# An attention-and-MLP kernel in which TensorE waits on its own products' counts instead of on a nop of another engine

## The chip, the cores and the metric

One core of a Trainium2 chip. Its engines are TensorE (PE in the profile, with weight loads as PEld), VectorE (DVE), ScalarE (ACT), GpSimd (POOL) and SyncE (SP), which issues nearly all DMA transfers here. Each engine works through a queue of its own in order; engines wait for one another through semaphores, which an instruction counts up when it completes. The metric is the time of one execution on the device in microseconds (us), the median of several runs. Engine names with a q, such as ACTq or PEldq, are the engine's queue: instructions that only wait, count or issue.

## What is computed

A transformer layer in which attention and MLP stand side by side, for 2048 tokens of width 512, 32 heads of width 16 and an MLP of width 1792, with fp32 input and output. Cut to what matters:

```
xn = layernorm(x)                                   # x: 1 x 2048 x 512
q, k, v = split_heads(xn @ wqkv)                    # 32 heads of 16
p = softmax(q @ k^T * 16 ** -0.5)                   # 2048 x 2048 for each head
attn = merge_heads(p @ v) @ wo
mlp = gelu_tanh(xn @ w1 + b1) @ w2 + b2             # 512 -> 1792 -> 512
out = x + attn + mlp
```

## The kernel before

**Number formats.** Operands of most products are split into a high and a low half-precision part; a dense product over one piece of its inner dimension is then three products (`PAIRS`, L155): high by high, high by low, low by high. Scores have the parts stacked in the inner dimension. Probabilities and V are fp32, and a product of those goes through the array in two passes.

**Stages.** A head of some 137 us prepares inputs and the first projections. Then one loop of units runs until close to the end. A unit has the attention work of one group of four heads, one block of 512 queries and one tile of 128 keys, and takes its dense work from a generator: first the other projections of q, k and v, then the MLP (for each of four blocks of 512 tokens: the first layer in 14 groups, then the second layer in four), and last the output projection, each as *groups* that fill one accumulator bank. Scores run 20 units (`LEAD`) ahead of the exponentials and P·V, because every row's maximum must be known before its exponentials: `s_half` (L214) makes scores with queries on partitions and VectorE takes their maximum (L226); `e_half` (L262) makes the same scores transposed, the maxima being in the operand as extra rows, and ScalarE takes the exponential from the bank (L273); `v_half` (L276) multiplies it with V.

**One block.** A unit has two half units, here *blocks*. The order is written by hand (a manual schedule: each engine's instructions stand in the order of the program). In a block TensorE gets

1. score products S, transposed scores T, S, T (one head each, in alternation on array rows 0 to 63 and 64 to 127);
2. four P·V products of an earlier unit's exponentials, on one row side `r`: each covers 64 keys and has 32 output columns of its own;
3. dense products on the other row side, `1 - r`, by `dense` (L532): three or four calls of `tiled` (L171) by the group's pace, each of four products with 32 columns of their own, so 12 or 16. `SLOW` is three calls in each block, `MEAN` three and four by turns, `FAST` four. The MLP's first layer alternates `SLOW` and `FAST` groups, its second layer has `SLOW` for the first two token blocks and `MEAN` for the last two; projections and output projection are `FAST`. A group ends after 6 blocks (`FAST`) or 8 (`SLOW`) in the first layer, after 28 (`SLOW`) or 24 (`MEAN`) in the second. In the block in which a new accumulation of P·V begins, dense products come first.

Both accumulators, one bank for P·V and one for the dense group, are fed from one row side in one block and from the other side in the next. Products on different row sides run at the same time on the array, so a block's P·V and dense products must not start before the last ones of the block before have finished: the order of instructions on TensorE alone does not give that.

**How that is kept.** All products go through `product` (L165), which keeps the newest one in `newest`. At the end of a block `unit` (L551) issues a nop (L579) on ScalarE or VectorE, whichever has the smaller backlog by the planner's account, and makes it depend on `newest` (L580). In the next block the first P·V or dense product (`fence[0]`, set at L566, used at L167) is made to wait for the nop. Whether a product counts for other readers (the reduction, the exponential, a buffer's next writer) is settled by the framework, which gives each instruction with a dependant on another engine its count.

**Buffers and loads the change touches.** `pe` (L271), the exponentials, has ten buffers; one is free once the P·V products that read it are done. `wc` (three buffers, weights of the first layer), `xb` (one buffer, a block of tokens) and `oc` (output projection) are read by dense products and loaded by SP. `stg` (L464) stages projections before they go to memory, `wo_l` (L95, loaded at L875) has a piece of the output weights for the tail.

Of the kernel before, what the change touches and what calls it, by code (L numbers as in the profile page):

```python
# [8 lines left out]
F32 = mybir.dt.float32  # L9
F16 = mybir.dt.float16  # L10
# [7 lines left out]
P = 128  # L18
S = 2048
D = 512  # L20
# [4 lines left out]
NC = D // P  # L25
NF = F // P
QB = 512
# [20 lines left out]
def layer_kernel(ctx: ExitStack, tc: tile.TileContext, x, wqkv, wo, w1, b1, w2, b2, out):  # L48
    nc = tc.nc
# [3 lines left out]
    def pool(stack, name, bufs=1, space=None):  # L53
        kw = {} if space is None else {"space": space}
        return stack.enter_context(tc.tile_pool(name=name, bufs=bufs, **kw))

    const = pool(ctx, "const")
# [34 lines left out]
    nc.gpsimd.memset(vv[:, :, 0:H * VW].rearrange("p t (h e) -> p t h e", e=VW)[:, :, :, DH], 1.0)  # L92
    nc.gpsimd.memset(vv[:, :, H * VW:], 0.0)
    wo_s = const.tile([P, 2, NC, D], F16, name="wo_s")
    wo_l = const.tile([64, 2, D], F16, name="wo_l")  # L95
    sexp = const.tile([P, 4], F32, name="sexp")

    mnegs = [const.tile([P, 32], F32, name=f"mneg{i}") for i in range(2)]
# [55 lines left out]

    PAIRS = ((0, 0), (0, 1), (1, 0))  # L155

    AFTER = mybir.DependencyInfo(mybir.DependencyClass.Sync, mybir.DependencyReason.DATA)
    fence, newest = [None], [None]

    backlog = {"act": 0, "dve": 0}  # L160

    def given(engine, ns):
        backlog[engine] += ns

    def product(*args, **kw):  # L165
        newest[0] = nc.tensor.matmul(*args, **kw)  # L166
        if fence[0] is not None:  # L167
            tc.add_manual_dep(newest[0].ins, fence[0].ins.name, AFTER, reason="other rows")
            fence[0] = None

    def tiled(dst, lhs, rhs, start, stop):  # L171

        for j in range(0, P, 32):
            product(dst[j:j + 32], lhs[:, j:j + 32], rhs, start=start, stop=stop)


    mt_of, ptiles, pv_of = {}, {}, {}
# [36 lines left out]
    def s_half(u, n):  # L214

        t, i = divmod(u, 16)
        g, qb = divmod(t, NQB)
        qt, kb = divmod(i, 4) if t else (i % 4, i // 4)
        if t not in mt_of:
            mt_of[t] = work.tile([P, 4, 4, 4], F32, name="mt", bufs=2)  # L220
        ks, qs = kst[g % 2], qst[g % 2]
        p, a = divmod(n, 2)
        r = slice(64 * a, 64 * a + 62)
        s = banks("S")
        tiled(s, qs[p][qb][r, qt * P:(qt + 1) * P], ks[p][kb][r, :], True, True)
        nc.vector.reduce_max(mt_of[t][:, n, qt, kb:kb + 1], s, axis=AX.X)  # L226
        given("dve", 600)

# [33 lines left out]
    def e_half(u, n):  # L262

        p, a = divmod(n, 2)
        t, kt = divmod(u, 16)
        g, qb = divmod(t, NQB)
        st = banks("T")
        r = slice(64 * a, 64 * a + 64)
        k0 = (kt % 4) * P
        tiled(st, kst[g % 2][p][kt // 4][r, k0:k0 + P], qst[g % 2][p][qb][r, :], True, True)  # L270
        pe = work.tile([P, QB], F32, name="pe", bufs=10)  # L271
        ptiles[u, n] = pe
        nc.scalar.activation(pe, st, AF.Exp, scale=sexp[:, g // 2:g // 2 + 1])  # L273
        given("act", 580)

    def v_half(u, a):  # L276

        t, kt = divmod(u, 16)
        g, qb = divmod(t, NQB)
        if kt == 0 and a == 0:  # L280
            pv_of[t] = hold("V", "S")
        pv = pv_of[t][0]
        r = slice(64 * a, 64 * a + 64)
        for h in (2, 3, 0, 1):
            c = (4 * g + h) * VW
            product(pv[32 * h:32 * h + 32, :], vv[r, kt, c:c + 32], ptiles[u, h][r],
                    start=(kt == 0 and a == 0), stop=(kt == 15 and a == 1))

    def v_end(u):
# [90 lines left out]
    class Group:  # L380
# [15 lines left out]
        def product(self, side):  # L396

            if self.bank is None:
                self.bank, self.key = self.alloc()
            lhs, rhs = self.prods[side % 2][self.at[side % 2]]()  # L400
            start = self.first and self.at == [0, 0]
            if side == 2:
                self.at = [min(self.at[0] + 1, n) for n in self.n]
                nc.tensor.matmul(self.bank, lhs, rhs, start=start, stop=self.last and self.over())  # L404
                return
            r = slice(64 * side, 64 * side + 64)
            self.at[side] += 1
            tiled(self.bank, lhs[r], rhs[r], start, self.last and self.over())

        def over(self):  # L410
            return self.at == self.n
# [40 lines left out]
    def project(m, w, sb, wh, bank, early=False):  # L452

        prods = [lambda c=c, i=i, j=j: (wh[:, w, i, c, :], xt[:, j, c, sb * QB:(sb + 1) * QB])
                 for c in range(NC) for i, j in PAIRS]

        dst = qk_d[w, m * P:(m + 1) * P, :, sb * QB:(sb + 1) * QB]

        def finish(pj):
            def put():  # L460
                nc.sync.dma_start(dst[:, w:w + 2, :], stg)
                nc.sync.dma_start(dst[:, 2 - 2 * w, :], stg[:, 0])

            stg = work.tile([P, 2, QB], F16, name="stg", bufs=2)  # L464
            given("act", 600)
            if early or (w == 1 and not m):
                nc.scalar.activation(stg[:, 0], pj, AF.Copy)
                nc.vector.tensor_tensor(stg[:, 1], pj, stg[:, 0], op=ALU.subtract)
            else:
                pf = ph.tile([P, QB], F32, name="pf", bufs=2)  # L470
                nc.scalar.activation(pf, pj, AF.Copy)
                if not m:
                    nc.scalar.activation(stg[:, 0], pj, AF.Copy)
                    nc.gpsimd.tensor_tensor(stg[:, 1], pf, stg[:, 0], op=ALU.subtract)
                else:
                    hi = lambda: nc.gpsimd.tensor_scalar(stg[:, 0], pf, 1.0, 0.0, op0=ALU.mult, op1=ALU.add)
                    lo = lambda: nc.gpsimd.tensor_tensor(stg[:, 1], pf, stg[:, 0], op=ALU.subtract)
                    later(1, lambda: pooled((620, hi), (1160, lo), (0, lambda: later(1, put, True))), True)
                    return

            put()

        return Group(prods, bank, finish)
# [62 lines left out]
                    cur[0].product(side)  # L546
        ended()

    passed_by = [None]

    def unit(gen):  # L551


        u = pos[0]
        e = u - LEAD
        if u == LEAD and cur[0] is not None:
            burst(gen, cur[0].left())
        pos[0] += 1
        for a in range(2):
            for b in range(2 * a, 2 * a + 2):  # L560
                if u < NU:
                    s_half(u, b)
                if 0 <= e < NU:
                    e_half(e, b ^ 1)
            if e >= 0:
                fence[0] = passed_by[0]  # L566

                w, r = (e - 2, 1) if a == 0 else (e - 1, 0)
                live = 0 <= w < NU
                new = r == 0 and w % 16 == 0  # L570
                if live and not new:
                    v_half(w, r)
                dense(gen, 1 - r)
                if live and new:
                    v_half(w, r)

                for k in backlog:
                    backlog[k] = max(0, backlog[k] - HALF)
                passed_by[0] = (nc.vector if backlog["dve"] < backlog["act"] else nc.scalar).nop()  # L579
                tc.add_manual_dep(passed_by[0].ins, newest[0].ins.name, AFTER, reason="block")  # L580
                if live and r == 1:
                    v_end(w)
                ended()
        if u < NU:
            s_end(u)
        if u < LEAD:
            burst(gen, LFILL[u - 16])
        tick()
# [9 lines left out]
    with ExitStack() as st1:  # L598
# [240 lines left out]
        def prepare():  # L839
# [20 lines left out]
            for n in range(16):  # L860
                v = fetch(16 + n)
                while not ended[0]:
                    yield
                ended[0] = False

                def then(wh=None, n=n):
                    ended[0] = True
                    if n < 7:
                        for a in range(2):
                            for l in range(2):  # L870
                                nc.sync.dma_start(w1_d[2 * n + a][:, l], wh[:, l, :, a * P:(a + 1) * P])
                    elif n < 14:
                        nc.sync.dma_start(w2_d[:, :, 2 * n - 14:2 * n - 12, :], wh)
                    elif n == 15:
                        nc.sync.dma_start(wo_l, wo_s[64:128, :, NC - 1, :])  # L875

                if n >= 14:
                    i = 2 * (n - 14)
                    split_steps(wo_s[:, 0, i:i + 2, :], wo_s[:, 1, i:i + 2, :], v, inv[:, 9:10], then)
                    continue  # L880
                wh = ph.tile([P, 2, 4, W] if n < 7 else [P, 2, 2, D], F16, name="wsp", bufs=2)
                k = n if n < 7 else 8
                split_steps(wh[:, 0], wh[:, 1], v, inv[:, k:k + 1], lambda wh=wh, then=then: then(wh))
# [150 lines left out]
        flush()  # L1034
    with ExitStack() as st3:
        p3 = pool(st3, "ph3")

        blocks = {}

# [64 lines left out]
```

## Time and profile before

| | |
|---|---|
| median of 3 runs | 1587.66 us (1586.63 to 1590.76) |
| the profiled execution | 1592.59 us |
| its span in the trace | 1590.8 us |
| granted TensorE clock, mean | 0.992 |
| blocks that end with a nop | 1027, from 137.3 to 1568.0 us |

The page of the profile begins with each engine's busy time, then shows the chain of work that ended last. Busy time is an average: matmul records overlap, since products on different pieces of the array run side by side, and an engine that is busy 97% of the span can still wait for something in every block. Rows of the timeline have start and length in us, then engine, line, operation, tiles (out<-in), partitions and elements, and the count of instructions gathered in the row; in brackets stands the engine's idle time before and what ended it. In views of waits the numbers are the total us, the times and the longest.

### The profile page before, as it was taken

The page shows a single profiled execution, that of the slowest core. Times are in us where ns is not written, and L with a number is a line of the kernel's source. Part 1 is how long each engine was busy: PE and PEld are TensorE (multiplying, and loading weights), DVE is VectorE, ACT ScalarE, POOL GpSimd, SP SyncE. Part 2 cuts the span into 40 slices and gives each one's busy share as a digit, 9 for nine tenths or more (in the row PEclk, how much of TensorE's full clock was granted, in tenths as well). Part 3 has the DMA queues.
Part 4 walks back from the last instruction along what each step waited for, and adds up shares of the span by engine and source line. Part 5 has one row for each costly group of instructions (what it writes and reads, how often), then busy time and mean ns, then how long its engine had stood idle before and what let it go on. Part 6 is the DMA issues. An engine that isn't in the chain of part 4 may idle for free.

```text
span 1590.8 us, 86996 instructions
## 1 busy us (share of the span) xinstructions
PE 1535.3 (97%) x38915; PEld 807.7 (51%) x38915; DVE 1424.0 (90%) x2388; ACT 1378.9 (87%) x2254; POOL 668.7 (42%) x742
## 2 busy tenths in 40 slices
PE   8997998999999999999999999999999999999998
PEld 4433554545555555555455555555555555554443
DVE  7896987989999999999899999999999999999901
ACT  4315997989999999999899999999999999999893
POOL 3113586727773111677411157681116775211000
PEclk9999999999999999999999999999999999999999
DMA  6466375361112111121111111221112110103222
GB/s 204 136 210 210 108 190 184 124 197 53 44 54 64 35 34 31 55 60 46 46 38 48 33 53 41 61 67 33 33 46 59 41 34 15 39 23 97 91 95 82
DMA packets 120256, 123.78 MB, mean 78 GB/s; under 512 B 38988, under 2 KB 90572, under 8 KB 119880
## 3 DMA queue, kind: packets, MB, share of 16 engines
q1 hardware_dynamic: 119880, 118.21, 24.6%
q8 instruction: 304, 4.98, 1.3%
q14 instruction: 72, 0.59, 0.1%
HBM read 80.61 MB, written 37.34 MB: 74 GB/s over the span
## 4 chain that ended last, share of the span: by engine, by line
PE 80%; DVE 10%; DMA 4%; POOL 2%; issue 2%; SPq 1%; ACT 1%; DVEq 0%; ACTq 0%; POOLq 0%
PE pV L166 25%; PE pD L166 18%; PE pT L166 17%; PE pS L166 16%; DVE mt L226 6%; DVE hh L955 2%; PE pD L404 1%; DMA wch<-in_B_w_dram 1%; PE pT L404 1%; DVE amx L614 1%; DMA dn<-den_d 1%; PE pT L497 1%; ACT pe L273 0%; DMA m_d<-mhl 0%; DMA xb<-xn_d 0%
## 5 line engine op out<-in xcount | busy, mean ns | idle before, releaser
L226 DVE TENSOR_REDUCE mt<-pS 128x1 f32<-128x512 f32 x2048 | 1293.2, 683 | 59.4 <-PE pS L166 34.3
L273 ACT ACTIVATE pe<-pT,sexp 128x512 f32<-128x512 f32 x2048 | 1270.1, 686 | 77.5 <-PE pT L166 27.9
L166 PE MATMUL pV<-pe,vv 64*32 64x512 f32 x8192 | 1083.3, 599 | 1.9 <-ACTq L579 0.8
L166 PE MATMUL pT<-qst,kst 64*32 64x512 f16 x8192 | 708.1, 379 | 11.3 <-DMA qst<-m_d 8.2
L166 PE MATMUL pS<-kst,qst 62*32 62x512 f16 x8192 | 640.9, 379 | 28.0 <-DVE mt L226 24.1
L166 PEld LDWEIGHTS <-qst 62*32 62x32 f16 x8192 | 271.5, 92 | 253.2 <-issue 123.0
L166 PEld LDWEIGHTS <-kst 64*32 64x32 f16 x8192 | 290.9, 91 | 209.4 <-issue 80.2
L166 PE MATMUL pD<-w_s,g 64*32 64x512 f16 x5376 | 365.4, 379 | 0.0
L166 PE MATMUL pD<-xb,wc 64*32 64x512 f16 x5376 | 360.9, 378 | 0.2 <-issue 0.2
L166 PEld LDWEIGHTS pV<-pe,vv 64*32 64x32 f32 x8192 | 177.0, 105 | 122.4 <-ACTq L579 25.4
L166 PEld LDWEIGHTS <-wc 64*32 64x32 f16 x5376 | 117.4, 92 | 46.0 <-issue 2.3
L166 PEld LDWEIGHTS <-g 64*32 64x32 f16 x5376 | 106.9, 92 | 44.2 <-issue 0.7
L166 PE MATMUL pD<-xt,wqk_h 64*32 64x512 f16 x1920 | 127.4, 381 | 0.7 <-issue 0.7
L973 POOL TENSOR_TENSOR xa<-xa,yt 128x512 f32<-128x512 f32 x16 | 20.4, 1276 | 242.9 <-ACT yt L971 242.9
L935 POOL TENSOR_TENSOR t<-hh 128x512 f32<-128x512 f32 x56 | 58.2, 1039 | 119.3 <-DVE hh L955 117.8
L324 POOL TENSOR_TENSOR osb<-osb,rb 128x512 f32<-128x512 f32 x31 | 39.8, 1284 | 157.0 <-DMA rb<-den_d 115.1
L250 POOL TENSOR_SCALAR mhl<-msb 64x64 f16<-64x64 f32 x32 | 7.6, 236 | 178.4 <-DVE msb L247 178.4
L937 POOL TENSOR_TENSOR t<-t,hh 128x512 f32<-128x512 f32 x56 | 71.7, 1280 | 4.7
L930 POOL TENSOR_TENSOR t<-t,hh 128x512 f32<-128x512 f32 x56 | 71.5, 1277 | 4.7
L932 POOL TENSOR_TENSOR g<-t,g 128x512 f16<-128x512 f32 x56 | 65.1, 1163 | 4.4
L166 PE MATMUL pD<-wo_s,oc 64*32 64x512 f16 x768 | 50.8, 378 | 0.8 <-issue 0.8
L166 PEld LDWEIGHTS <-wqk_h 64*32 64x32 f16 x1920 | 43.0, 92 | 16.7 <-issue 1.9
(138 smaller groups left out, 868.0 us busy)
## 6 DMA issues: line engine op xcount, KB each, us to landing
wch<-in_B_w_dram SPq DMA_DIRECT2D x28, 512.0 KB
wc<-w_d SPq DMA_DIRECT2D x56, 256.0 KB
qk_d<-stg SPq DMA_DIRECT2D x32, 256.0 KB
rb<-den_d SPq DMA_DIRECT2D x124, 64.0 KB
kst<-qk_d SPq DMA_DIRECT2D x128, 48.0 KB
qst<-qk_d SPq DMA_DIRECT2D x128, 48.0 KB
xs<-in_A_x_dram SPq DMA_DIRECT2D x16, 256.0 KB
qk_d<-stg SPq DMA_DIRECT2D x32, 128.0 KB
```

The lines of the kernel that those rows point to most:

```text
L166: newest[0] = nc.tensor.matmul(*args, **kw)
L226: nc.vector.reduce_max(mt_of[t][:, n, qt, kb:kb + 1], s, axis=AX.X)
L273: nc.scalar.activation(pe, st, AF.Exp, scale=sexp[:, g // 2:g // 2 + 1])
L324: pooled((1280, lambda: nc.gpsimd.tensor_tensor(osb, osb, rb, op=ALU.mult)), (620, lambda: nc.gpsimd.tensor_scalar(ot[:, 0], osb, 1.0, 0.0 ...
L404: nc.tensor.matmul(self.bank, lhs, rhs, start=start, stop=self.last and self.over())
L497: nc.tensor.matmul(pj, xt[:, i, c, t * P:(t + 1) * P], wh[j][:, c, :], start=(n == 0), stop=(n == 11))
L930: (1280, lambda: nc.gpsimd.tensor_tensor(t1, t1, hh, op=ALU.mult)),
L932: (1160, lambda: nc.gpsimd.tensor_tensor(g[:, 1, f, :], t1, g[:, 0, f, :], op=ALU.subtract)),
L935: pooled((1040, lambda: nc.gpsimd.tensor_tensor(t1, hh, hh, op=ALU.mult)), (620, lambda: nc.gpsimd.tensor_scalar(t1, t1, 1.0, 1.0 / GELU_A ...
L937: (1280, lambda: nc.gpsimd.tensor_tensor(t1, t1, hh, op=ALU.mult)),
L955: nc.vector.tensor_scalar(hh, hp, scale, bias, op0=ALU.mult, op1=ALU.add)
L973: add = lambda: nc.gpsimd.tensor_tensor(xa, xa, yt, op=ALU.add)
```

## The change

The nop of the other engine goes. Each P·V product carries a key of its kind and head, each dense product one of its kind and column piece, score products none. At the end of a block `leave` takes the newest product of each key, so the four last P·V and the four last dense products, and makes each count a semaphore `turns` up by one when it completes; it does so only where the accumulation goes on in the next block. In the next block `enter` puts one instruction on TensorE's queue that waits until `turns` has reached the number counted so far. It is also declared to the framework as the point after which those products are done; who reuses their operands' buffers waits for that point. The exponentials get twelve buffers instead of ten. `stg` moves to the pool of the first stage, and `wo_l` with its load to the last stage.

```diff
-    wo_l = const.tile([64, 2, D], F16, name="wo_l")
...
-    AFTER = mybir.DependencyInfo(mybir.DependencyClass.Sync, mybir.DependencyReason.DATA)
-    fence, newest = [None], [None]
...
-    def product(*args, **kw):
-        newest[0] = nc.tensor.matmul(*args, **kw)
-        if fence[0] is not None:
-            tc.add_manual_dep(newest[0].ins, fence[0].ins.name, AFTER, reason="other rows")
-            fence[0] = None
-
-    def tiled(dst, lhs, rhs, start, stop):
+    turns = tc.alloc_semaphore("turns")
+    counted, waits, newest = [0], [[]], {}
+
+    def product(key, *args, **kw):
+
+        p = nc.tensor.matmul(*args, **kw)
+        if key[0] is not None:
+            newest[key] = p
+
+    def leave(user, goes_on):
+
+        for key in [k for k in newest if k[0] == user]:
+            p = newest.pop(key)
+            if goes_on:
+                p.then_inc(turns, 1)
+                tc.no_tile_sem_insts.add(p.ins.name)
+                counted[0] += 1
+                waits[0].append(p)
+
+    def enter():
+
+        if waits[0]:
+            group = f"turn{counted[0]}"
+            for p in waits[0]:
+                tc.add_to_no_dep_group(group, p.ins)
+            w = nc.tensor.wait_ge(turns, counted[0])
+            tc.declare_fence(w.ins, group=group)
+            waits[0] = []
+
+    def tiled(user, dst, lhs, rhs, start, stop):
 
         for j in range(0, P, 32):
-            product(dst[j:j + 32], lhs[:, j:j + 32], rhs, start=start, stop=stop)
+            product((user, j), dst[j:j + 32], lhs[:, j:j + 32], rhs, start=start, stop=stop)
...
-        pe = work.tile([P, QB], F32, name="pe", bufs=10)
+        pe = work.tile([P, QB], F32, name="pe", bufs=12)
...
-            product(pv[32 * h:32 * h + 32, :], vv[r, kt, c:c + 32], ptiles[u, h][r],
+            product(("V", h), pv[32 * h:32 * h + 32, :], vv[r, kt, c:c + 32], ptiles[u, h][r],
...
-            stg = work.tile([P, 2, QB], F16, name="stg", bufs=2)
+            stg = ph.tile([P, 2, QB], F16, name="stg", bufs=2)
...
-                fence[0] = passed_by[0]
+                enter()
...
+                for user, goes_on in (("V", live and not (r == 1 and w % 16 == 15)),
+                                      ("D", cur[0] is not None and not cur[0].over())):
+                    leave(user, goes_on)
                 for k in backlog:
                     backlog[k] = max(0, backlog[k] - HALF)
-                passed_by[0] = (nc.vector if backlog["dve"] < backlog["act"] else nc.scalar).nop()
-                tc.add_manual_dep(passed_by[0].ins, newest[0].ins.name, AFTER, reason="block")
...
-                    elif n == 15:
-                        nc.sync.dma_start(wo_l, wo_s[64:128, :, NC - 1, :])
...
         p3 = pool(st3, "ph3")
+        wo_l = p3.tile([64, 2, D], F16, name="wo_l")
+        nc.sync.dma_start(wo_l, wo_s[64:128, :, NC - 1, :])
```

More of the change, by code (lines that the diff above doesn't have):

```diff
@@ L224, in s_half @@
         s = banks("S")
-        tiled(s, qs[p][qb][r, qt * P:(qt + 1) * P], ks[p][kb][r, :], True, True)
+        tiled(None, s, qs[p][qb][r, qt * P:(qt + 1) * P], ks[p][kb][r, :], True, True)
         nc.vector.reduce_max(mt_of[t][:, n, qt, kb:kb + 1], s, axis=AX.X)
@@ L269, in e_half @@
         k0 = (kt % 4) * P
-        tiled(st, kst[g % 2][p][kt // 4][r, k0:k0 + P], qst[g % 2][p][qb][r, :], True, True)
-        pe = work.tile([P, QB], F32, name="pe", bufs=10)
+        tiled(None, st, kst[g % 2][p][kt // 4][r, k0:k0 + P], qst[g % 2][p][qb][r, :], True, True)
+        pe = work.tile([P, QB], F32, name="pe", bufs=12)
         ptiles[u, n] = pe
@@ L407, in product @@
             self.at[side] += 1
-            tiled(self.bank, lhs[r], rhs[r], start, self.last and self.over())
+            tiled("D", self.bank, lhs[r], rhs[r], start, self.last and self.over())
         def over(self):
@@ L547, in land @@
         ended()
-    passed_by = [None]
     def unit(gen):
```

## The prediction

> **What bounds the kernel now.** The page's busy shares and its chain of waits came first.
>
> ```profile
> span 1590.8 us, 86996 instructions
> PE 1535.3 (97%) x38915; PEld 807.7 (51%) x38915; DVE 1424.0 (90%) x2388; ACT 1378.9 (87%) x2254; POOL 668.7 (42%) x742
> PE 80%; DVE 10%; DMA 4%; POOL 2%; issue 2%; SPq 1%; ACT 1%; DVEq 0%; ACTq 0%; POOLq 0%
> PE pV L166 25%; PE pD L166 18%; PE pT L166 17%; PE pS L166 16%; DVE mt L226 6%; DVE hh L955 2%; PE pD L404 1%; DMA wch<-in_B_w_dram 1%; PE pT L404 1%; DVE amx L614 1%; DMA dn<-den_d 1%; PE pT L497 1%; ACT pe L273 0%; DMA m_d<-mhl 0%; DMA xb<-xn_d 0%
> ```
>
> The products of L166 carry 76% of the chain. But four of them run side by side on pieces of the array, so 97% busy does not say that the array is full. What matters is the period of a block (half a unit), so I then counted exponentials (two to a block) by stage.
>
> ```profile
> 160.00:317.20 157.20, 129.78 (x211) 0.98 0.51 152
> 333.10:472.20 139.10, 120.17 (x195) 1.00 0.26 77
> 473.50:621.90 148.40, 138.62 (x223) 1.00 0.15 43
> 622.90:759.70 136.80, 120.39 (x195) 1.00 0.19 52
> 760.50:914.60 154.10, 138.37 (x223) 0.98 0.14 42
> 915.70:1053.30 137.60, 120.55 (x195) 1.00 0.18 52
> 1054.10:1182.30 128.20, 118.83 (x191) 1.00 0.14 42
> 1183.30:1319.00 135.70, 120.44 (x195) 1.00 0.16 45
> 1319.80:1448.10 128.30, 118.87 (x191) 1.00 0.09 24
> 1448.80:1463.10 14.30, 13.71 (x25) 1.00 0.30 91
> 1465.60:1501.10 35.50, 30.15 (x49) 1.00 0.41 132
> 1513.50:1563.90 50.40, 47.51 (x77) 1.00 0.26 84
> ```
>
> The columns are the stretch, its length, ScalarE's busy time and count at the exponential L273, the granted clock, DMA share and rate. The first stretch is the projections. The four with x195 are the MLP's first layer (549.2 us, 390 blocks, 1.41 us each). The two with x223 are its second layer at the slow pace (302.5 us, 223 blocks, 1.36), the two with x191 the same at the mean pace (256.5 us, 191 blocks, 1.34). The last three are attention and output projection.
>
> What holds a block at these periods is seen in the timeline, rows being start, length, engine and operation: a block with twelve dense products, one with sixteen, and two with none.
>
> ```profile
> 563.65 0.63 PE L166 MATMUL pV<-pe,vv 64*32 64x512 f32 x4
> 563.68 0.61 PE L166 MATMUL pD<-w_s,g 64*32 64x512 f16 x8
> ...
> 564.10 0.61 PE L166 MATMUL pV<-pe,vv 64*32 64x512 f32 x4
> 564.12 0.39 PE L166 MATMUL pD<-w_s,g 64*32 64x512 f16 x4
> ...
> 564.94 0.63 PE L166 MATMUL pV<-pe,vv 64*32 64x512 f32 x4
> ```
>
> ```profile
> 1546.92 0.64 PE L166 MATMUL pV<-pe,vv 64*32 64x512 f32 x4
> ...
> 1546.95 0.61 PE L166 MATMUL pS<-wo_s,oc 64*32 64x512 f16 x8
> ...
> 1548.25 0.63 PE L166 MATMUL pV<-pe,vv 64*32 64x512 f32 x4
> ```
>
> ```profile
> 1460.27 3.07 DVE L226 TENSOR_REDUCE mt<-pS 128x1 f32<-128x512 f32 x5
> ...
> 1460.72 0.63 PE L166 MATMUL pV<-pe,vv 64*32 64x512 f32 x4
> ...
> 1461.17 0.61 PE L166 MATMUL pV<-pe,vv 64*32 64x512 f32 x4
> ...
> 1461.92 0.63 PE L166 MATMUL pV<-pe,vv 64*32 64x512 f32 x4
> ```
>
> With no dense product the P·V pair (two passes) ends at 1461.17+0.61 = 1461.78 and the next begins 0.14 later: a period of 1.20. With twelve dense products the second pass ends at 564.71, the dense ones before it, and yet the next begins only 0.23 later: a period of 1.29 (1.30 with rounding). With sixteen it is 1.33. So a dense product costs the period 0.10/12 or 0.13/16, some 8 ns, though its work is done in time: the products' completions seem to be counted one after another, in program order. The loop that binds is thus P·V, its completion and those of the dense products behind it, the count, the nop, the next P·V. VectorE is the nearest other limit: five reductions in 3.07 with the last 0.68 long give 0.60 each, 1.20 per block.
>
> ```profile
> L579 ACTq EVENT_SEMAPHORE  x1027: 17/17/17, 137.3 to 1568.0; - x172
> ...
>   PEld pV L166: 26.8, 75
> ```
>
> This view of the nop's line shows that all 1027 waits stand on ScalarE, and that TensorE's weight loads wait for them.
>
> **The change part by part.** *Removed*: 1027 nops at 17 ns, 17 us of ScalarE. ScalarE is 1% of the chain, so as ScalarE's work they are worth nothing; what they cost TensorE is a part of the 0.14 hop. *Added*: a stand-alone wait on TensorE's own queue per block. The trace has just one like it.
>
> ```profile
> L355 PEldq EVENT_SEMAPHORE  x1: 51/51/51, 1570.4 to 1570.4; - x1
> ```
>
> ```profile
> 1569.97 0.42 DVE L352 TENSOR_TENSOR on<-pS,rden 128x256 f32<-128x256 f32 x1
> 1570.51 0.14 PEld L355 LDWEIGHTS pS<-ident,on 128*64 128x64 f32 x2 [1.10 <-PE pS L349]
> ```
>
> VectorE ends at 1570.39 and the load begins 0.12 later. The nop's whole path took 0.14. So one wait of 51 ns replaces a nop of 17 ns and one crossing. By ends alone it could save 0.02; by the two waits' lengths, with no crossing saved, it costs 51−17 = 34 ns. I take +0.03, since those 51 are time of TensorE's queue itself, and keep −0.02 to +0.05 (the 51 whole). Behind it in TensorE's queue stand the same loads and score products as behind the waiting load of before, so nothing else is held up.
>
> *Moved*: the counting. Before, a block had one count for this purpose, on its newest product. After, the last four P·V products and the last four dense products each count: eight. What a count costs is read where two counts stand four products apart.
>
> ```profile
> 481.02 0.39 PE L166 MATMUL pS<-kst,qst 62*32 62x512 f16 x1 [0.84 <-issue]
> 481.03 0.40 PE L166 MATMUL pT<-qst,kst 64*32 64x512 f16 x4
> ...
> 481.45 0.69 DVE L226 TENSOR_REDUCE mt<-pS 128x1 f32<-128x512 f32 x1 [0.78 <-PE pT L166]
> 481.51 0.69 ACT L273 ACTIVATE pe<-pT,sexp 128x512 f32<-128x512 f32 x1 [0.72 <-PE pT L166]
> ```
>
> Score products on both row sides begin together (481.02, 481.03); both consumers had been idle, and they begin 60 ns apart. Four products at 8.3 ns make 33 of that, so the count itself is 27 ns; with products at 7.5 to 9 ns it is 24 to 30. I take 26. Bounds: nothing, if counts of side-by-side products are passed on at once, and the whole 60.
>
> The Trainium skill (TensorE: Matmul & The Clock Gate, section "The cost: per-tile semaphore tail") speaks against the change: completion increments of array tiles are written one after another, about 26.3 ns each beside 4.7 ns per tile, and since products complete in order a single increment on the last is enough. By it seven more would take 0.184 us, an estimate from that page. The trace agrees on the count (27) and not on the tile (8.3); that four side-by-side products queue for their counts no row shows.
>
> So a block whose dense group goes on gets 7×0.026+0.03 = +0.21: 1.51 with twelve products, 1.54 with sixteen. One without dense products gets 3×0.026+0.03 = +0.11, 1.31. One in which the group ends waits only for P·V's four counts, which stand ahead of the dense ones: also 1.31. At these periods VectorE's 1.20 (with L955 in one block of seven, some 1.3) is hidden, and small stalls of today go under:
>
> ```profile
> PE pS L166 <- DVE mt L226: 24.1, 32, 8.7
> PEld L166 <- DMA qst<-m_d: 12.7, 7, 4.0
> ```
>
> The sum against the profiled execution, 1592.6 (its span 1590.8 and 1.8 around it):
> - First layer: of 14 blocks seven at 1.51, five at 1.54, two at 1.31, mean 1.492; 390×1.492 = 581.9 against 549.2: +32.7.
> - Second layer, slow: (27×1.51+1.31)/28 = 1.503; 223×1.503 = 335.2 against 302.5: +32.7.
> - Second layer, mean pace (12 and 16 by turns): (23×1.525+1.31)/24 = 1.516; 191×1.516 = 289.6 against 256.5: +33.1.
> - Last stretch, (5×1.54+1.31)/6 = 1.502; 38.5×1.502 = 57.8 against 50.4: +7.4. The 24.5 blocks of the stretch before it, which has other waits, get the same rise without them, 0.17: +4.2.
> - The 12.5 blocks of the short stretch and the 42 between the stretches (1027 less 985), mostly without dense products: 54.5×0.11 = +6.0.
> - Projections: 157.2/105.5 = 1.49 already against 1.50 by rows. Other waits hold them (DMA share 0.51), and part of the rise comes on top: I take 0.05 a block, +5.3 (0 to 0.21, so 0 to 22).
>
> In the first layer the rows alone make 1.31 a block now, of 1.41; I let that 0.10 of other waits go under. If it stays, 390×0.10 = 39 come on top (1748).
>
> Together +121: 1714 for the profiled execution. That one stood 4.9 over the median of 1587.7, so the median comes to 1709.
>
> *At nothing*: the exponential buffers come free one block later, through the next block's wait, and twelve for ten cover two blocks' use; were that cover gone, an exponential would start late by up to its own 0.69 (row 481.51) in a block. The wc tiles, freed in the same way, have three buffers and are loaded two groups, some 14 blocks, ahead. The load of wo_l moves from SP's queue in stage one to the head of stage three, one issue ahead of the oc loads, and stg moves to the stage's pool, which holds the xb load back behind the last stores and four qst loads: below nothing no reason, above at most the 12.7 us that loads wait for DMA qst<-m_d today; I take 0, since each is once in the run.
>
> **The rivals.**
> *Counts do not queue.* Counts of products on different columns pass side by side. For it: the row shows only two counts, of consecutive groups. Against: dense products that ended early still cost 8 ns each, so something is taken in turn. Then only the hop is left: 985×0.03 = +30, 1618.
> *Faster: the crossing saved.* The 0.14 from P·V's end to the next holds two crossings, to ScalarE and back; TensorE's own wait needs one. If half of it goes, 0.07 is saved in the 223+191+38.5+54.5 = 507 blocks where nothing else is near (−35) and some 0.02 in the first layer's 390, where VectorE's 1.3 is near (−8): 1545. It decides if eight counts cost less than 10 ns each. For it: the 26.8 us in 75 rows in which loads wait for the nop. Against: the stand-alone wait's 51 ns and 0.12.
> *Each count costs the whole 60.* 7×0.06+0.03 = +0.45 in some 930 blocks: about 2005. Against: the periods with 12 and 16 products.
> *It changes nothing*: what the wait saves, the counts take, 1588.
>
> **How the numbers follow.** The forecast has 0.68: two kinds of row give its price, and the loop's periods fit without a rest. Its own range: the block's rise is 0.14 (counts of 23, hop −0.02) to 0.26 (30, +0.05) for 0.21, so 0.07 less or 0.05 more in some 970 blocks: 1641 to 1758. Counts that do not queue, or only in part, have 0.15; the saved crossing 0.10; the 60 0.04; no change 0.03. The range for 8 in 10 goes from 1605, which takes in the second case, to 1755; outside lie the saved crossing, no change, the 60 and a little of the first. Faster by over 0.3% (5 us, about what a measurement of this kernel can tell) 0.10, within it 0.03, slower 0.87.
>
> **What would show it.** After, the timeline of the slow second layer has P·V starts about 1.51 apart, the second pass ending some 0.44 before the next (0.23 now), and blocks with no dense product 1.31 apart. The two x223 stretches last some 168 us each at equal clock, the first layer's some 145. The weight load waits for TensorE's own wait, and VectorE's and ScalarE's idle time goes up with PE named as releaser. The prediction is wrong if twelve-product blocks stay at or under 1.35: then the counts are free and the hop decides. If blocks keep their period and the rise sits at exponentials waiting for buffers, or at xb, oc or wo_l loads, the mechanism is another.

## The result, and the profile after

The changed kernel took 1776.15 us (median of 4 runs, 1768.82 to 1783.87) against 1589.21 for the kernel before in the same comparison: a ratio of 1.118 (1.113 to 1.123). It is slower, as forecast, but by 187 us where 121 were forecast, and outside the range. The page of the profiled execution (1777.21 us, its span in the first line):

```profile
span 1775.4 us, 87004 instructions
...
PE 1701.3 (96%) x38915; PEld 869.1 (49%) x38915; DVE 1443.7 (81%) x2388; ACT 1396.0 (79%) x2254; POOL 669.2 (38%) x742
...
PE 36%; DVE 2%; issue 1%; POOL 0%; SPq 0%; DMA 0%; DVEq 0%; POOLq 0%
```

Work is the same (38915 products on TensorE); VectorE's share falls from 90% to 81%, ScalarE's from 87% to 79%. So these two wait more, and TensorE sets the pace. The chain of waits breaks off and covers only 40% of the span here; it can't be compared with the one before. Its place is taken by the stretches with the same exponentials in them (line 273 is now 295; columns as before):

```profile
161.20:338.70 177.50, 131.62 (x210) 0.99 0.46 133
353.00:509.80 156.80, 122.68 (x194) 0.99 0.25 73
511.70:687.10 175.40, 140.38 (x223) 1.00 0.12 36
688.20:841.20 153.00, 123.36 (x195) 1.00 0.16 47
842.30:1012.50 170.20, 140.69 (x223) 1.00 0.13 38
1013.80:1164.60 150.80, 122.82 (x195) 1.00 0.16 47
1165.60:1314.30 148.70, 120.25 (x191) 1.00 0.13 36
1315.40:1467.10 151.70, 123.11 (x195) 1.00 0.15 40
1468.10:1616.50 148.40, 120.47 (x191) 1.00 0.07 21
1617.30:1632.80 15.50, 14.21 (x24) 1.00 0.39 117
1635.70:1676.40 40.70, 30.44 (x48) 1.00 0.31 99
1689.60:1748.30 58.70, 48.15 (x77) 1.00 0.21 67
```

| stage | before | forecast rise | measured rise |
|---|---|---|---|
| projections | 157.2 | 5.3 | 20.3 |
| first layer, four stretches | 549.2 | 32.7 | 63.1 |
| second layer, slow pace | 302.5 | 32.7 | 43.1 |
| second layer, mean pace | 256.5 | 33.1 | 40.6 |
| last two stretches | 85.9 | 11.6 | 13.5 |

The granted clock is the same within 0.02. Every stage is longer, and the forecast is close where the blocks were even before (the last stretches), far off where other waits had lain between them. The timeline of after shows the single block. First one with twelve dense products, then one with sixteen, then one with none:

```profile
1429.90 0.63 PE L169 MATMUL pV<-pe,vv 64*32 64x512 f32 x4
...
1430.37 0.59 PE L169 MATMUL pV<-pe,vv 64*32 64x512 f32 x1
...
1431.39 0.63 PE L169 MATMUL pV<-pe,vv 64*32 64x512 f32 x4
```

```profile
1700.35 0.63 PE L169 MATMUL pV<-pe,vv 64*32 64x512 f32 x4
...
1701.88 0.63 PE L169 MATMUL pV<-pe,vv 64*32 64x512 f32 x4 [0.21 <-PE pD L169]
```

```profile
1629.20 0.63 PE L169 MATMUL pV<-pe,vv 64*32 64x512 f32 x4
...
1630.49 0.63 PE L169 MATMUL pV<-pe,vv 64*32 64x512 f32 x4
```

The periods are 1.49 (forecast 1.51), 1.53 (1.54) and 1.29 (1.31). In the first, the second pass ends at 1430.96 and the next block begins 0.43 later, 0.23 before. So the price of a block was forecast well, and yet the sum was 66 us short. The wait, in the view of its line and in the view of all waits:

```profile
L189 PEldq EVENT_SEMAPHORE  x1027: 51/51/51, 138.9 to 1753.1; - x172
```

```profile
PEld pV L169 <- issue: 263.6, 831, 3.1
...
DVE mt L248 <- PE pS L169: 118.2, 350, 4.8
```

All 1027 waits stand alone, 51 ns each. "issue" is time in which a unit waited for nothing that the profile shows: P·V's weight loads stand still 831 times for 264 us in all, and no releaser is named; what stands ahead of them is the wait, an instruction of TensorE's own queue. VectorE's waits for scores rose to 118.2 us; before, the same view had

```profile
DVE mt L226 <- PE pS L166: 34.3, 84, 3.6
```

as its row for them.

### The profile page after: what moved, and what is told of

Its sections match the earlier page's. It is cut to its first block, busy times and chain, and to the rows that moved or that the text cites. A ratio compares the mean times of both kernels' runs of the same rounds, so it can differ in the third digit from the quotient of the medians.

```text
span 1775.4 us, 87004 instructions
## 1 busy us (share of the span) xinstructions
PE 1701.3 (96%) x38915; PEld 869.1 (49%) x38915; DVE 1443.7 (81%) x2388; ACT 1396.0 (79%) x2254; POOL 669.2 (38%) x742
## 5 line engine op out<-in xcount | busy, mean ns | idle before, releaser
L295 ACT ACTIVATE pe<-pT,sexp 128x512 f32<-128x512 f32 x2048 | 1291.9, 686 | 254.7 <-ACT pe L295 114.5
L248 DVE TENSOR_REDUCE mt<-pS 128x1 f32<-128x512 f32 x2048 | 1309.4, 684 | 207.1 <-PE pS L169 118.2
L169 PE MATMUL pV<-pe,vv 64*32 64x512 f32 x8192 | 1117.8, 598 | 15.7 <-issue 7.3
L169 PE MATMUL pT<-qst,kst 64*32 64x512 f16 x8192 | 745.0, 378 | 10.7 <-issue 9.2
L169 PE MATMUL pS<-kst,qst 62*32 62x512 f16 x8192 | 682.0, 379 | 31.6 <-DVE mt L248 23.2
L169 PEld LDWEIGHTS <-kst 64*32 64x32 f16 x8192 | 312.3, 91 | 185.6 <-issue 46.3
L169 PEld LDWEIGHTS <-qst 62*32 62x32 f16 x8192 | 284.6, 92 | 229.3 <-issue 95.7
L169 PE MATMUL pD<-xb,wc 64*32 64x512 f16 x5376 | 368.0, 379 | 2.4 <-DMA kst<-qk_d 1.9
L169 PEld LDWEIGHTS pV<-pe,vv 64*32 64x32 f32 x8192 | 203.5, 104 | 274.0 <-issue 263.6
L974 DVE TENSOR_SCALAR hh<-pD,fac,b_s 128x512 f32<-128x512 f32 x56 | 45.3, 810 | 8.9 <-PE pT L169 1.8
```

What stands on the lines that cost most here:

```text
L169: p = nc.tensor.matmul(*args, **kw)
L974: nc.vector.tensor_scalar(hh, hp, scale, bias, op0=ALU.mult, op1=ALU.add)
```

## Experiments

All ratios are against the kernel before on the same chip. Periods are those of most blocks of a kind in the whole trace, from the start of one P·V to the next. The code is cut to the lines that matter.

**How much is the counting?** In `one`, only the newest product of those that the next block waits for counts; in `two`, the last P·V and the last dense product; in `all`, every dense product and the four of P·V.

```diff
 # one: in place of the eight counts of leave()
+                if newest:
+                    p = list(newest.values())[-1]
+                    p.then_inc(turns, 1)
+                    counted[0] += 1
...
 # two
+                    for p in {k[0]: q for k, q in newest.items()}.values():
+                        p.then_inc(turns, 1)
+                        counted[0] += 1
...
 # all
-            product((user, j), dst[j:j + 32], lhs[:, j:j + 32], rhs, start=start, stop=stop)
+            product((user, j, len(newest)), dst[j:j + 32], lhs[:, j:j + 32], rhs, start=start, stop=stop)
```

> Only the newest product of a block that another waits for counts on the semaphore: one count for eight; the stand-alone wait, the fence, twelve buffers and the moved loads stay. Theory 1, each count costs 26 ns in the loop and the wait itself 18 ns more than the nop (from 1.495 against 1.29 with eight counts, and 1.292 against 1.196 with four): blocks with twelve dense products 1.31 to 1.33, with sixteen 1.34 to 1.36, total 1600 to 1620. Theory 2, most of the rise comes from the stand-alone wait or from buffers freed a block later: twelve-product blocks over 1.40, total over 1680.

> The last P*V product and the last dense product count: two for eight. Theory 1: one count more than with a single one, 26 ns a block, twelve-product blocks 1.33 to 1.36, total 20 to 28 us over the single count. Theory 2: no different from the single count.

> Every dense product of the block counts, twelve or sixteen, beside the four of P*V: eight or twelve counts more than the changed kernel. Theory 1: twelve-product blocks 1.495+8*0.026 = 1.70, with sixteen 1.529+12*0.026 = 1.84, total 1950 to 2010. Theory 2: within 20 us of the changed kernel's 1776.

Measured: one 1653.8 (1.039, 1.037 to 1.042), two 1678.4 (1.052, 1.049 to 1.056), all 1944.3 (1.220, 1.218 to 1.223). P·V starts of twelve-product blocks in the timelines of one, of two and of all:

```profile
805.80 0.63 PE L169 MATMUL pV<-pe,vv 64*32 64x512 f32 x4
...
807.13 0.63 PE L169 MATMUL pV<-pe,vv 64*32 64x512 f32 x4
```

```profile
806.48 0.63 PE L169 MATMUL pV<-pe,vv 64*32 64x512 f32 x4
...
807.84 0.63 PE L169 MATMUL pV<-pe,vv 64*32 64x512 f32 x4
```

```profile
607.64 0.63 PE L169 MATMUL pV<-pe,vv 64*32 64x512 f32 x4 [0.20 <-PE pV L169]
...
609.34 0.63 PE L169 MATMUL pV<-pe,vv 64*32 64x512 f32 x4 [0.20 <-PE pV L169]
```

1.33, 1.36 and 1.70. In most blocks of the traces it is 1.332, 1.358, 1.495 (the change) and 1.702: one count more is 26 ns, eight more are 207, 26 each. With sixteen dense products it is 1.529 and 1.839: twelve more are 310, again 26. So the forecast's price holds for a further count on a dense product. From the single count to the change's eight it is a little high: 0.163 for seven, 23 each, and in blocks without dense products three more on P·V are 0.059 (1.233 to 1.292), 20 each. The periods came out as theory 1 had them, and all's total was 6 us under its range. But the single count, for which theory 1 asked 1600 to 1620, took 1654: something beside the counts costs 60 us.

**The counts alone, with the nop.** Seven dense products of a block, not the last ones, count on a semaphore that nobody reads. They do so only where the dense group goes on.

```diff
+                for p in dense_of[:-4][:7] if cur[0] is not None and not cur[0].over() and live and not new else []:
+                    p.then_inc(idle, 1)
...
```

> The kernel before, with its nop, its ten buffers and its loads, but seven other dense products of a block count on a semaphore that nobody waits for (861 of 1027 blocks). Theory 1: blocks with twelve 1.29+7*0.026 = 1.47 to 1.49, total 1715 to 1770. Theory 2: under 1620, for counts are not what costs.

Measured: 1704.7 (1.070, 1.068 to 1.072). Two P·V starts, and two stretches of it (projections, and the last of the first layer):

```profile
508.95 0.63 PE L167 MATMUL pV<-pe,vv 64*32 64x512 f32 x4
...
510.43 0.63 PE L167 MATMUL pV<-pe,vv 64*32 64x512 f32 x4
```

```profile
161.60:326.00 164.40, 130.88 (x210) 0.98 0.50 145
...
1262.10:1408.10 146.00, 121.61 (x195) 1.00 0.16 42
```

The period is 1.476 in most blocks, against 1.295 before (1.289 and 1.302 by turns): (1.476−1.295)/7 = 26 ns a count. The total came out under the expectation, since the rise was taken up in part: the projections rose by 7 us where the blocks alone would give 861/1027 of 105×0.181, some 16. With the nop in place, the forecast's idea that a longer block swallows other waits is right.

**The moved pieces.** In `moves`, only the twelve buffers, stg's pool and wo_l's load are changed; in `one_unstg`, `one` has stg back in the common pool (`on`, a small tile of the tail, shares an exponential's buffer).

```diff
 # moves, against the kernel before
+        pe = work.tile([P, QB], F32, name="pe", bufs=12)
+            stg = ph.tile([P, 2, QB], F16, name="stg", bufs=2)
+        wo_l = p3.tile([64, 2, D], F16, name="wo_l")
 # one_unstg, against one
+            stg = work.tile([P, 2, QB], F16, name="stg", bufs=2)
```

> The kernel before with its nops, but with twelve exponential buffers, stg in the stage's pool and wo_l loaded in the last stage, as the change has them. The prediction: nothing, 1590 to 1597. Theory 3: a part of what counts and wait don't explain lies here, since with a single count the run fell 7 to 9 us behind in the first 15 us of the MLP's first layer, where xb is loaded: 1600 to 1612, the step at the same place.

> The single count with stg back in the common pool (a small tile of the tail shares an exponential's buffer to make the room). Theory 3: the step at the start of the first layer goes, 1638 to 1647 against 1654 with the single count. Rival, that stg's pool is nothing: 1650 to 1657.

Measured: 1593.5 (0.999, 0.998 to 1.000) and 1659.5 (1.040, 1.038 to 1.043). Theory 3 falls: the moves are worth nothing, as forecast, and stg's old place brings nothing back (1659.5 is even 2.5 us over what its rival allowed).

**VectorE's 0.81 at a group's turn.** In the first layer, the block after a group's end takes 1.7 to 1.8 before and after the change. Both runs do VectorE's piece for 8 of its 512 columns and leave out the rest.

```diff
-                    nc.vector.tensor_scalar(hh, hp, scale, bias, op0=ALU.mult, op1=ALU.add)
+                    nc.vector.tensor_scalar(hh[:, :8], hp[:, :8], scale, bias, op0=ALU.mult, op1=ALU.add)
```

> The changed kernel, with the evacuation of the first layer (L974, 0.81 us of VectorE once a group) done for 8 of 512 columns; the rest of hidden units is left at a constant. Theory 4: the long block at each group's turn (1.7 to 1.8 for 1.5) is VectorE's 0.81 in one piece, which slack of other blocks cannot take in advance: it shrinks to 1.55 or less, first layer windows 0.02 to 0.03 shorter per block, total 1755 to 1768. Rival, the turn is held by loads or the accumulator bank: unchanged, 1770 to 1782.

> The same cut in the kernel before. Theory 4: 56 turns give back 0.25 to 0.4 each, 1570 to 1580. Rival: 1586 to 1597.

Measured: 1779.1 (1.115, 1.112 to 1.119) and 1578.8 (0.990, 0.987 to 0.993). In the kernel before, theory 4 holds: the block after a group's end goes from 1.70 to 1.44 in the median, and 56 turns give back 15 us. In the changed kernel it goes from 1.78 to 1.53, as theory 4 said, and yet the total did not move: what was gained at the turns was lost in other blocks. So there VectorE's piece is not what the total hangs on, and theory 4 does not explain the missing 66 us.

**Where the wait stands.** In `one_att` and `after_att`, the wait is not an instruction of its own but is put on the block's first P·V or dense product, which is also declared as the point after which buffers come free (this product itself does not count, so `after_att` has seven counts). In `nop_pe`, the kernel before gets a nop on TensorE's queue that waits for ScalarE's nop.

```diff
 # one_att and after_att: product() and enter()
+        if key[0] is not None and pend[0] is not None:
+            value, group = pend[0]
+            pend[0] = None
+            p._wait_ge(turns, value)
+            tc.declare_fence(p.ins, group=group)
+            gate[0] = p
...
-            w = nc.tensor.wait_ge(turns, counted[0])
-            tc.declare_fence(w.ins, group=group)
+            pend[0] = counted[0], group
...
 # nop_pe, against the kernel before
-                fence[0] = passed_by[0]
...
+                    turn_nop = nc.tensor.nop()
+                    tc.add_manual_dep(turn_nop.ins, passed_by[0].ins.name, AFTER, reason="other rows")
```

> The single count, but the wait stands on the first P*V or dense product of the block itself, not in an instruction of its own; that product is the point after which buffers come free. Theory 5: the stand-alone wait makes the 0.04 a block and the extra stalls (107 us over the blocks' floor against 82 before), so both go and the nop's way through ScalarE is saved too: twelve-product blocks 1.22 to 1.30, total 1555 to 1600. Rival 6, buffers freed at the next block's point, or the count of a product itself: 1635 to 1660, blocks 1.33.

> The kernel before with its nop on ScalarE, and a stand-alone instruction on TensorE's queue that waits for it in place of the first product; buffers and counts as before. Theory 5: 0.04 to 0.10 a block and more stalls, 1640 to 1700. Rival 6: 1590 to 1605.

> The changed kernel with the wait on the first product of the block (that one doesn't count, so seven counts). Theory 5: twelve-product blocks 1.40 to 1.45, stalls over the floor 10 to 25 us as with the seven idle counts, total 1660 to 1705. Rival 6: 1735 to 1776.

Measured: one_att 1566.6 (0.984, 0.981 to 0.986), nop_pe 1591.2 (0.999, 0.998 to 1.001), after_att 1651.8 (1.038, 1.035 to 1.040). P·V starts of twelve-product blocks in one_att, then in after_att:

```profile
486.96 0.63 PE L170 MATMUL pV<-pe,vv 64*32 64x512 f32 x4
...
487.42 0.61 PE L170 MATMUL pV<-pe,vv 64*32 64x512 f32 x4
...
488.23 0.64 PE L170 MATMUL pV<-pe,vv 64*32 64x512 f32 x4
```

```profile
620.29 0.63 PE L170 MATMUL pV<-pe,vv 64*32 64x512 f32 x4
...
621.70 0.63 PE L170 MATMUL pV<-pe,vv 64*32 64x512 f32 x4
```

In most blocks 1.263 and 1.405. Against the same kernels with the wait by itself (1.332, 1.495), a block is 0.069 shorter with one count; with eight it is 0.090, of which one count is up to 0.026, so at least 0.064. Over some 1000 blocks that is 66 us of the 87 between one and one_att, and of the 124 between the change and after_att. The traces show where it sits. In most twelve-product blocks the next P·V's first weight load begins 0.402 us after the end of P·V's last product in the change and 0.341 in after_att, one count included, and the product itself begins 0.031 after its load in the change and 0.002 in after_att. In one and one_att the whole way from P·V's end to the next product is 0.270 and 0.201. One_att is the fastest kernel of this study. Theory 5's ranges held for it; after_att's block of 1.405 was in its range too, its total 8 us below. The nop's way over ScalarE cost 0.03 a block (1.263 for 1.295), and the wait of TensorE on itself is worth it if it is carried by a product and there is one count.

The run nop_pe settles nothing about the wait. The view of its nop's line:

```profile
L567 PEldq EVENT_SEMAPHORE  x1: 51/51/51, 1567.6 to 1567.6; - x1
```

One instruction stood alone; the others were gone from the trace, their waits being on the products as before, so that the program ran as before. Hence the last run: the nop counts a semaphore, and TensorE's wait for it counts another, as the change's wait does, so that it stays an instruction.

```diff
-                fence[0] = passed_by[0]
...
+                    w_ = nc.tensor.wait_ge(hop, hops[0])
+                    w_.then_inc(gone, 1)
...
+                passed_by[0].then_inc(hop, 1)
```

> Theory 5 by itself, since in the run with the nop on TensorE's queue the wait came out on the block's first product and nothing stood alone: the kernel before with its nop, ten buffers and loads, the nop counting a semaphore, and an instruction of its own on TensorE's queue that waits for it and counts one that nobody reads. No product counts more than before and no buffer is freed later. Theory 5: the instruction costs the 0.064 to 0.069 a block by which the changed kernel and the single count differ from their versions without it, so twelve-product blocks 1.35 to 1.37, total 1650 to 1695 with up to 25 us of added stalls. Rival 6, the wait is dear only where buffers hang on it: 1590 to 1610.

Measured: 1705.3 (1.072, 1.069 to 1.075). Two P·V starts, the wait's line, the waits, and the same two stretches as above:

```profile
694.83 0.63 PE L168 MATMUL pV<-pe,vv 64*32 64x512 f32 x4
...
696.20 0.63 PE L168 MATMUL pV<-pe,vv 64*32 64x512 f32 x4
```

```profile
L569 PEldq EVENT_SEMAPHORE  x1027: 51/51/51, 138.1 to 1676.4; - x172
```

```profile
PEld pV L168 <- issue: 211.9, 854, 2.8
```

```profile
159.90:333.60 173.70, 130.76 (x210) 1.00 0.48 137
...
1260.70:1405.20 144.50, 120.98 (x195) 1.00 0.16 42
```

The period is 1.377 in most blocks, 0.08 over the kernel before: 82 us in 1027 blocks. The rest of the 114 is added stalls, in projections above all: 16.5 us longer, while the 0.08 would give some 8. Period and total lie a little above theory 5's ranges (1.37, 1695) and far from rival 6. No buffer hangs on this wait and no product counts more. Theory 5 stands, and the wait by itself costs as much as seven counts do (111). The loads' "issue" time is back as well. In one_att, the longest wait of these loads is

```profile
PEld pV L170 <- PE pS L170: 7.2, 14, 0.7
```

with a releaser named.

## Why the prediction came out as it did

**What bounds, and a block's price: right.** The loop of P·V, counts in order and the next P·V was read correctly, and the forecast of +0.21, +0.21 and +0.11 compares with +0.20, +0.20 and +0.10 measured. A further count on a dense product is 26 ns, as taken; the change's seven were 0.163 in all where 0.182 were taken. The rivals "counts do not queue" and "each costs 60" are refuted by two, all and the idle counts. The rule of the Trainium skill that the prediction weighed (TensorE: Matmul & The Clock Gate, section "The cost: per-tile semaphore tail") agrees on the count, 26.3 ns for 26 measured, and in what it advises: with the last product alone counting, 122 us of the change's time go. Its 4.7 ns per tile differ from the trace, where four more dense products make (1.529−1.495)/4 = 8.5 ns each.

**The wait: taken well as a sum, misread as parts.** The forecast had +0.03 for the wait in place of the nop; it is +0.037 (with the single count, 1.233 against 1.196 without dense products, 1.332 against 1.295 with twelve). It holds a saving of some 0.03 for the nop's way and a cost of 0.064 to 0.08 for the instruction by itself. The forecast read −0.02 to +0.05 from one row of 51 ns and one gap of 0.12, and took 51−17 with no crossing saved; that its +0.03 came so near is luck, for it had the saving at nothing and the instruction at half its price. The saved crossing of the faster rival exists, then, but not in this kernel: it needs the wait on a product.

**What failed: "small stalls of today go under", and with it "so nothing else is held up".** The forecast let the first layer's 0.10 a block of other waits, the second layer's smaller ones, and most of the projections' vanish under a longer block. It also took TensorE's own wait to hold up nothing that the waiting load of before had not held up. The term is what a trace has over its blocks' usual periods, summed over the whole trace: each block's P·V start to the next, less the usual one for twelve, sixteen or no dense products. Blocks in which a group ends have a usual period of their own (1.292 with twelve and 1.336 with sixteen in the change, where they wait for fewer counts). Counted so, the sums are higher than the 107 and 82 that an expectation above names. Each row is one execution, up to 10 us from its kernel's median.

| kernel | wait | usual period, 12 dense | stalls over it, us |
|---|---|---|---|
| one_att | on a product | 1.263 | 104 |
| before | on a product, behind the nop | 1.295 | 89 |
| after_att, seven counts | on a product | 1.405 | 59 |
| before with seven idle counts | on a product, behind the nop | 1.476 | 39 |
| one | by itself | 1.332 | 128 |
| two | by itself | 1.358 | 121 |
| nop and wait by itself | by itself | 1.377 | 114 |
| the change | by itself | 1.495 | 91 |

Where a product carries the wait, stalls do go under as the block grows: 89 us to 39 at 1.476. With the wait by itself they are some 40 to 60 us more at like periods, so the change keeps all that there were before, 91 for 89. Of the profiled executions' 184.6 us, the usual periods make 182.5. The forecast's own prices, put on the same blocks, make 193, ten more than measured; it booked 121 and so let 72 vanish, of which none did, and that is the difference. By stage, it shows in the first layer (30 us over the forecast), the projections (15) and the second layer (18), the places where the forecast had named other waits. The reserve that it kept for the first layer, "if it stays, 39 come on top", was the right case; with the same reserve in every stage the sum would have come close to the result.

**At nothing: right.** Moved loads, stg and twelve buffers are worth nothing (moves). The lines by which the prediction was to be tested fit: P·V 0.43 before the next (forecast 0.44), blocks without dense products 1.29; the slow stretches of 175 and 170 us passed the forecast's 168, and the first layer's of 151 to 157 its 145, by their stalls.

**What stays open.** Why a wait that stands alone lets more stalls through is seen only in part. In 69 blocks of the change, 94 of one and 58 of the last run the first four products of P·V begin over 0.1 us apart, against 9 before and 8 in one_att. These blocks make 31, 31 and 28 us of their kernels' stalls, against 2.5 and 1.9. So about half of the added stalls sits there; why the products come apart is open, and so is the other half. The time that P·V's loads put to "issue" tells nothing of it, for with seven idle counts, where stalls are 39 us, they stand still nearly as long, with the nop's wait named:

```profile
PEld pV L167 <- ACTq L589: 223.9, 712, 0.9
```

Whether the instruction is dear because it waits alone or because it counts as well was not separated: without its own count, it did not stay an instruction.

## What to carry to other kernels

Where products of several array tiles are followed by a wait, let one product count, the last in order, and let the wait ride on the first product that needs it: eight counts for one cost 122 us here, and the wait by itself 87 to 114. A nop on another engine is a dear way to wait only next to that; it was 26 us slower than the best form and 187 better than the change. And when a sum lets small stalls vanish under a longer period, price the case that they stay in every stage, for what is added may itself make stalls.

## What was not expected of the hardware

A wait of 51 ns by itself on TensorE's queue lengthened the loop by 0.064 to 0.08 us against the same wait on a product, more than a second hop over ScalarE with its 17 ns nop (0.03). In the change, against after_att, its price sat in two places: the weight load behind it came 0.035 later (0.061 with one count of 0.026), and the product 0.029 later after that load. A further count on a dense product was 26 ns, as the one more of two as well as for each of the twelve more on top of eight, and whether or not anybody waited for it; three more on P·V products were 20 each.
